# The first weight's fp16 parts without POOL, the low part of P in column halves, and a plan with new times

## Chip, core and metric

The kernel runs on one core of a Trainium2 chip. The metric is the device time of one execution in microseconds; it is given as the median of several runs.

## What is computed

Clustered attention is followed by a feed-forward block. The attention has 4 batches, 8 heads, 768 positions and a head dimension of 64. Cut to what matters:

```
q_assign = argmax(q_n . c_n)      # each query's cluster, of 16; k_assign likewise
mask     = q_assign == k_assign
scores   = where(mask, q k^T / 8, -1e9)
attn     = softmax(scores)
x        = (attn v) laid out as 3072 tokens x 512
h        = x @ w_in               # 512 x 2048
g        = h * tanh(softplus(h))
out      = g @ w_out              # 2048 x 512
```

## The kernel before

**Precision by two fp16 parts.** Nearly every matmul operand after the scores is split into a high fp16 part and a low fp16 part (what is left over), and products of parts are summed in PSUM. A feed-forward product takes three matmuls: high x high, high x low and low x high (lines 687 to 689 for w_in, 725 to 727 for w_out).

**Units.** The work of attention is cut into 96 units: 32 pairs of batch and head, three blocks of 256 queries each. A unit has two halves `a` of 128 queries. For each half TensorE makes scores (lines 520 and 525), VectorE the row's maximum (`rowmax`, line 535), ScalarE the exponentials P and their sum l (`expo`, line 542), and `recip` turns l into a factor (lines 552 and 553; the first step of it on POOL or VectorE). The page and the views call VectorE DVE, ScalarE ACT and GpSimd POOL.

- In the first 24 units (batch 0) P stays fp32 and is transposed on TensorE (line 581) and copied out of PSUM by DVE (line 600) or ACT (line 602). `pv` then multiplies it with an fp32 V of 64 columns (line 620). Two units share one PSUM bank: one writes partitions 0 to 63, the other 64 to 127. Their matmuls stand in turn in the queue, so each uses 64 of the array's columns ("128*64" in the profile). Line 641 spreads the factors in the same manner.
- In the other 72 units `p_hi` and `p_lo` make the parts of P (lines 571 and 588), one DMA transposes both, and `pv` runs once for two units, 36 times in all: for each unit 12 matmuls of line 630, six blocks of keys by two parts of P. The stationary operand is 128 columns wide, V's high part and V's low part side by side; the moving one is 256 queries. Rows 0 to 63 of the result hold what V's high part gives, rows 64 to 127 what its low part gives, and `pv_out` adds the two (lines 664 and 665).

**The weights.** `w_load`, `w_abs` (ACT, line 243) and `w_f32` (DVE, lines 256 and 258) turn 32 tiles that arrive as 64-bit words into fp32; `w_sq` sums their squares on TensorE (line 273) for a scale. Then come, for each of 16 column blocks, `w_hi` and `w_lo`, the fp16 parts. Blocks 0 to 7 are w_in, 8 to 15 w_out. There are two ways for a block. In one, POOL writes both parts (lines 297 and 306) after a scaling on POOL or ACT (lines 294 and 296). In the other, ACT writes the high part (line 291) and DVE the low part (line 304). The table's `f_w` says how many blocks go the second way; before, none of the first weight's did. `w_hi` of a block overwrites what `w_lo` of the block ahead of it has read, so the steps alternate.

**The order.** `Plan` holds each step with a due time, counted in units. `run` issues the steps in the order of these times, each after what it needs, and a scheduler then lays down each engine's queue from that. The times, and the shares of the steps that go to one engine or another (`share`: a share of 1 or more, or of -1 or less, takes every one), stand in the table `T` at the end of the file. Steps of the feed-forward are due one for each unit from 25.4 on; what is left of them when attention ends runs alone at the end.

Of the kernel before, what the change touches and what calls it, by code (L numbers as in the profile page):

```python
# [18 lines left out]
B, H, S, D, NCL = 4, 8, 768, 64, 16  # L19
# [36 lines left out]
def tile_clustered_attention_mish_ffn(  # L56
# [9 lines left out]
    nc = tc.nc  # L66
# [20 lines left out]
    st = {}  # L87
# [32 lines left out]
    units = [(g, qb, g) for g in range(NG) for qb in range(3)]  # L120
# [188 lines left out]
    vst = {}  # L309
# [245 lines left out]
    def mode(i, a):  # L555


        n, late = 2 * i + a, i >= T["units0"]
        if i < 3 * H:
            return 3  # L560
        return 2 if share(n, "f_lo", late) else int(share(n, "f_hi", late))
# [46 lines left out]
    def pv(m):  # L608

        for i in (2 * m, 2 * m + 1):  # L610
            b, h = divmod(units[i][0], H)
            pl.after(("ptrans", i, 0), ("ptrans", i, 1), ("v_split", b, h // 2))
        o = ps2.tile([P, 512], F32, tag="M", name=f"o{m}", bufs=1)
        early = mode(2 * m, 0) == 3
        if early:

            for c in range(6):
                for s in range(2):
                    b, h = divmod(units[2 * m + s][0], H)
                    nc.tensor.matmul(  # L620
                        o[s * D : s * D + D, :256], vst[b, h // 2][:, c, h % 2], st["pt", 2 * m + s][:, :, c, :],
                        start=(c == 0), stop=(c == 5), skip_group_check=True,
                    )
        else:

            for s in range(2):
                b, h = divmod(units[2 * m + s][0], H)
                for c in range(6):
                    for part in range(2):
                        nc.tensor.matmul(  # L630
                            o[:, s * 256 : s * 256 + 256], vst[b, h // 2][:, c, h % 2].rearrange("p g d -> p (g d)"),
                            st["pt", 2 * m + s][:, :, c + 6 * part, :],
                            start=(part == 0 and c == 0), stop=(part == 1 and c == 5), skip_group_check=True,
                        )
        if early:

            for s in range(2):
                for a in range(2):
                    pl.after(("recip", 2 * m + s, a))
                    c0 = 256 + a * P  # L640
                    nc.tensor.matmul(
                        o[s * D : s * D + D, c0 : c0 + P], st["l", 2 * m + s, a].to_broadcast([P, D]), ident,
                        start=True, stop=True, skip_group_check=True,
                    )
        st["o", m] = o
# [122 lines left out]
    for n in range(32):  # L768
        p = n // 16
# [5 lines left out]
    for i in range(16):  # L775
        p = i // 8
# [7 lines left out]
    for n in range(1, NG):  # L784

        span = T["span", int(n >= H)]
# [25 lines left out]
    for i in range(NU):  # L812
        for a in range(2):
            pl.at(i + T["scores", a], scores, i, a)
            pl.at(i + T["rowmax", a], rowmax, i, a)
            pl.at(i + T["expo", a], expo, i, a)
            pl.at(i + T["recip", a], recip, i, a)
            q = "q" if mode(i, a) == 3 else "p"
            pl.at(i + T[f"{q}_hi", a], p_hi, i, a)
            pl.at(i + T[f"{q}_lo", a], p_lo, i, a)  # L820
            pl.at(i + T[f"{q}_trans", a], ptrans, i, a)
        if i % 2:
            pl.at(i + T["pv"], pv, i // 2)
            pl.at(i + T["pv_out"], pv_out, i - 1)
            pl.at(i + T["pv_out"], pv_out, i)
# [17 lines left out]

T = {
    ('f_ws', 0): 0.5,
    ('f_ws', 1): 0.5,
    'direct': 2,
    'free': 6,
    't0': 2.1861,
    ('f_pl', 0): 0.5,  # L850
    ('as_o', 0): 0,
    ('as_o', 1): 0,
# [6 lines left out]
    ('dq', 'copy_z'): 0,  # L859
    ('dq', 'copy_b'): -9,  # L860
    ('dq', 'copy_a'): 0,
    ('f_copy_t', 0): 0,
    ('f_copy_z', 0): 0.567,
    ('f_copy_b', 0): 0,
    ('f_copy_a', 0): 0,
    ('f_copy_t', 1): 3,
    ('f_copy_z', 1): 0.874,
    ('f_copy_b', 1): 0,
    ('f_copy_a', 1): 0.193,
    ('f_a', 0): 1,  # L870
    ('f_a', 1): 0.239,
    ('f_b', 0): -1,
    ('f_b', 1): 0,
    'prep_hi': 3.0343,
    'prep_lo': 1.1321,
    'copy_t': 0.5952,
    'copy_z': 0.8008,
    'copy_b': 3.5728,
    'copy_a': 1.7632,
    'hot_copy': 0.979,  # L880
    'm_store': 0.3296,
    ('f_l', 0): 0,
    ('f_l', 1): 0.434,
    ('w_l', 0): 0.8888,
    ('w_l', 1): 0.7772,
    'v0': 2.031,
    'v_d': 0.4275,
    ('q_hi', 0): 0.8,
    ('q_lo', 0): 1.4045,
    ('q_trans', 0): -0.3083,  # L890
    ('q_hi', 1): 1.3,
    ('q_lo', 1): 1.5418,
    ('q_trans', 1): 1.5,
    ('f_w', 0): 0,
    ('f_w', 1): 0.363,
    'lead': 0.5333,
    'units0': 24,
    ('f_d', 0): 0.965,
    ('f_d', 1): 0.732,
    ('f_lo', 0): 0,  # L900
    ('f_lo', 1): 0,
    ('f_hi', 0): 0,
    ('f_hi', 1): 1,
    'grp': 2,
    'mish': 0,
    'O': 1,
    'off0': 25.401,
    'pace': 1.0,
    ('span', 0): 1.1575,
    ('span', 1): 1.0762,  # L910
    ('load', 0): -3.8837,
    ('load', 1): 2.8849,
    ('w0', 0): 0.89,
    ('w0', 1): 9.896,
    ('w_d', 0): 0.3597,
    ('w_d', 1): 0.1964,
    ('ws0', 0): 4.1159,
    ('ws0', 1): 1.7919,
    ('ws1', 0): -0.216,
    ('ws1', 1): 2.5545,  # L920
    ('ws_d', 0): 0.7109,
    ('ws_d', 1): 1.2087,
    'assign': 0.2164,
    'hot': 2.2946,
    'put': 2.3669,
    ('scores', 0): 0.4,
    ('rowmax', 0): 0.9821,
    ('expo', 0): 2.0645,
    ('recip', 0): 0.7,
    ('scores', 1): 1.8591,  # L930
    ('rowmax', 1): 1.6368,
    ('expo', 1): 1.1,
    ('recip', 1): 1.0726,
    ('p_hi', 0): 0.611,
    ('p_lo', 0): 0.9,
    ('p_trans', 0): 1.0,
    ('p_hi', 1): 1.3,
    ('p_lo', 1): 1.2157,
    ('p_trans', 1): 1.5,
    'pv': 3.4,  # L940
    'pv_out': 3.6,
    'm2': 4.327,
    'm_out': 0.4,
}

# [27 lines left out]
```

## Time and profile before

| | us |
|---|---|
| median of 3 runs (970.0 to 970.25) | 970.15 |
| the profiled execution | 970.7 |
| its span, first to last instruction | 968.9 |

So 1.8 us of the profiled execution lie outside its span, and it took 0.55 us longer than the median. A line of a view that groups instructions gives the source line, engine, operation, output and input, shapes and count; then the busy time in us and the mean duration of one in ns; then the idle time of the engine just before them and what ended it. "PEld" is TensorE's weight load. Matmuls are pipelined, so the duration of one is longer than the distance to the next one; the distance is what a stream of them costs. Shapes of a matmul are rows*columns of the array, then partitions x elements of the output or of the moving operand.

### The profile page before, as it was taken

The page shows a single profiled execution, that of the slowest core. Times are in us where ns is not written, and L with a number is a line of the kernel's source. Part 1 is how long each engine was busy: PE and PEld are TensorE (multiplying, and loading weights), DVE is VectorE, ACT ScalarE, POOL GpSimd, SP SyncE. Part 2 cuts the span into 40 slices and gives each one's busy share as a digit, 9 for nine tenths or more (in the row PEclk, how much of TensorE's full clock was granted, in tenths as well). Part 3 has the DMA queues.
Part 4 walks back from the last instruction along what each step waited for, and adds up shares of the span by engine and source line. Part 5 has one row for each costly group of instructions (what it writes and reads, how often), then busy time and mean ns, then how long its engine had stood idle before and what let it go on. Part 6 is the DMA issues. An engine that isn't in the chain of part 4 may idle for free. (4 is left out here: it accounts for less than half of the span.)

```text
span 968.9 us, 17115 instructions
## 1 busy us (share of the span) xinstructions
PE 906.2 (94%) x6385; PEld 668.9 (69%) x6385; DVE 648.8 (67%) x1169; ACT 554.2 (57%) x940; POOL 410.8 (42%) x542
## 2 busy tenths in 40 slices
PE   4788679999899999999999999899999999999997
PEld 3665456777677777667777767677777777666663
DVE  6897997887777767867776767877777766111010
ACT  4666367777666766566677656566666664211111
POOL 3227749744354444544444335544444343211110
PEclk9999789999999999999999999999999999999999
DMA  9733542246777857577785766578778666000000
GB/s 359 252 85 89 178 127 63 70 101 120 148 158 135 162 114 145 124 125 149 122 161 127 156 136 146 100 143 127 151 129 131 125 107 114 25 12 23 12 12 22
DMA packets 256083, 115.85 MB, mean 120 GB/s; under 512 B 230592, under 2 KB 236352, under 8 KB 256000
## 3 DMA queue, kind: packets, MB, share of 16 engines
q1 hardware_dynamic: 244320, 83.29, 43.8%
q10 hardware_dynamic: 11680, 31.46, 12.0%
q8 instruction: 50, 0.82, 0.4%
q14 instruction: 33, 0.27, 0.1%
HBM read 35.68 MB, written 6.29 MB: 43 GB/s over the span
## 5 line engine op out<-in xcount | busy, mean ns | idle before, releaser
L542 ACT ACTIVATE p<-s,m 128x768 f32<-128x768 f32 x192 | 172.9, 901 | 131.9 <-DVE m L535 108.2
L688 PE MATMUL h<-x,w 128*128 128x256 f16 x768 | 209.9, 273 | 1.1 <-POOL x L669 1.1
L687 PE MATMUL h<-x,w 128*128 128x256 f16 x768 | 210.0, 274 | 0.5 <-ACT u L697 0.5
L689 PE MATMUL h<-x,w 128*128 128x256 f16 x768 | 210.2, 274 | 0.0
L588 DVE SCALAR_TENSOR_TENSOR hl<-p,l,hl 128x768 f16<-128x768 f32 x144 | 152.8, 1063 | 64.2 <-POOL hl L571 63.3
L535 DVE TENSOR_REDUCE m<-s 128x1 f32<-128x768 f32 x192 | 181.1, 945 | 6.0 <-PE s L525 4.9
L571 POOL TENSOR_SCALAR hl<-p,l 128x768 f16<-128x768 f32 x144 | 133.5, 928 | 115.6 <-ACT p L542 38.2
L709 DVE SCALAR_TENSOR_TENSOR g<-u,mscg,g 128x512 f16<-128x512 f32 x96 | 76.2, 796 | 139.0 <-POOL g L701 138.4
L701 POOL TENSOR_SCALAR g<-u,mscg 128x512 f16<-128x512 f32 x96 | 82.4, 859 | 174.4 <-ACT u L697 148.9
L725 PE MATMUL O<-w,g 128*128 128x512 f16 x384 | 146.3, 381 | 2.2 <-POOL g L701 1.4
L727 PE MATMUL O<-w,g 128*128 128x512 f16 x384 | 145.7, 379 | 0.2 <-DVE g L709 0.2
L726 PE MATMUL O<-w,g 128*128 128x512 f16 x384 | 145.7, 380 | 0.0
L520 PE MATMUL s<-A,B 128*128 128x384 f32 x384 | 122.5, 400 | 15.5 <-ACT p L542 12.9
L697 ACT ACTIVATE u<-h,msch 128x512 f32<-128x512 f32 x96 | 65.8, 687 | 98.5 <-PE h L689 93.2
L630 PE MATMUL o<-pt,v 128*128 128x256 f16 x864 | 103.2, 273 | 1.0 <-DMA pt<-hl 0.4
L525 PE MATMUL s<-Z,T 80*128 80x384 f32 x384 | 100.5, 344 | 2.5 <-issue 1.9
L552 POOL TENSOR_SCALAR l<-l 128x1 f32<-128x1 f32 x129 | 39.6, 307 | 148.5 <-ACT p L542 145.2
L630 PEld LDWEIGHTS <-v 128*128 128x128 f16 x864 | 83.9, 98 | 18.5 <-issue 2.0
L687 PEld LDWEIGHTS <-w 128*128 128x128 f16 x768 | 75.3, 98 | 19.4 <-issue 5.5
L520 PEld LDWEIGHTS s<-A,B 128*128 128x128 f32 x384 | 63.3, 193 | 34.6 <-ACT p L542 20.0
L688 PEld LDWEIGHTS <-w 128*128 128x128 f16 x768 | 75.4, 98 | 17.0 <-issue 2.8
L689 PEld LDWEIGHTS <-w 128*128 128x128 f16 x768 | 75.4, 98 | 14.9 <-issue 5.4
(184 smaller groups left out, 1300.2 us busy)
## 6 DMA issues: line engine op xcount, KB each, us to landing
qk<-in_qk_dram ACTq DMA_DIRECT2D x30, 384.0 KB, 4.1
stage<-in_w_out_dram ACTq DMA_DIRECT2D x16, 512.0 KB, 4.9
vraw<-in_vP_dram SPq DMA_DIRECT2D x16, 384.0 KB, 4.0
out_dram<-osb SPq DMA_DIRECT2D x24, 256.0 KB, 2.2
B<-T ACTq DMA_DIRECT2D x30, 192.0 KB, 4.2
A<-A SPq DMA_DIRECT2D x25, 192.0 KB, 4.8
stage<-in_w_in_dram SPq DMA_DIRECT2D x8, 512.0 KB, 8.6
stage<-in_w_in_dram ACTq DMA_DIRECT2D x8, 512.0 KB, 4.6
```

The costliest lines, as they stand in the source:

```text
L520: nc.tensor.matmul(s[:, j, :384], st["B", n][:, q0 : q0 + P], st["A", n][:, j * 384 : (j + 1) * 384], start=True, stop=False,)
L535: nc.vector.tensor_reduce(m, st["s", i, a][:, :, :384], axis=AX.XY, op=ALU.max, negate=True)
L542: in_turn(nc.scalar.activation(p.rearrange("p (n x) -> p n x", n=2), st["s", i, a][:, :, :384], AF.Exp, bias=st["m", i, a], scale=1.0, acc ...
L571: nc.gpsimd.tensor_scalar(t[:, 0], p, r, 1.0, op0=ALU.mult, op1=ALU.mult)
L588: nc.vector.scalar_tensor_tensor(t[:, 1], p, r, t[:, 0], op0=ALU.mult, op1=ALU.subtract)
L630: nc.tensor.matmul(o[:, s * 256 : s * 256 + 256], vst[b, h // 2][:, c, h % 2].rearrange("p g d -> p (g d)"), st["pt", 2 * m + s][:, :, c + ...
L687: nc.tensor.matmul(o, wh, xh, start=(c == 0), stop=False)
L688: nc.tensor.matmul(o, wh, xl, start=False, stop=False)
L689: nc.tensor.matmul(o, wl, xh, start=False, stop=(c == 3))
L725: nc.tensor.matmul(o, gh, wh, start=(f == 0 and fi == 0), stop=False)
L726: nc.tensor.matmul(o, gh, wl, start=False, stop=False)
L727: nc.tensor.matmul(o, gl, wh, start=False, stop=(f == 7 and fi == 1))
```

## The change

In `pv`, for the 72 later units, the two kinds of matmul are parted. The 12 with P's high part stay as they were, those of the first unit and then those of the second. The 12 with P's low part take V's high part alone, a stationary operand of 64 columns, and the two units stand in turn: the first writes partitions 0 to 63, the second 64 to 127, each in its own 256 columns of the bank. The product of the two low parts is no longer computed. Only the first matmul of a block now starts the bank afresh, and the first of the second unit is placed behind it.

```diff
+            vs = [vst[b, h // 2][:, :, h % 2] for b, h in (divmod(units[2 * m + s][0], H) for s in range(2))]
+            pts = [st["pt", 2 * m + s] for s in range(2)]
             for s in range(2):
-                b, h = divmod(units[2 * m + s][0], H)
                 for c in range(6):
-                    for part in range(2):
-                        nc.tensor.matmul(
-                            o[:, s * 256 : s * 256 + 256], vst[b, h // 2][:, c, h % 2].rearrange("p g d -> p (g d)"),
-                            st["pt", 2 * m + s][:, :, c + 6 * part, :],
-                            start=(part == 0 and c == 0), stop=(part == 1 and c == 5), skip_group_check=True,
-                        )
+                    mm = nc.tensor.matmul(
+                        o[:, s * 256 : s * 256 + 256], vs[s][:, c].rearrange("p g d -> p (g d)"),
+                        pts[s][:, :, c, :], start=(s == 0 and c == 0), stop=False, skip_group_check=True,
+                    )
+                    if c == 0:
+                        if s:
+                            behind(mm, begun, "one start for the bank")
+                        begun = mm.ins.name
+
+            for c in range(6):
+                for s in range(2):
+                    nc.tensor.matmul(
+                        o[s * D : s * D + D, s * 256 : s * 256 + 256], vs[s][:, c, 0],
+                        pts[s][:, :, 6 + c, :], start=False, stop=(c == 5), skip_group_check=True,
+                    )
...
-    ('f_w', 0): 0,
+    ('f_w', 0): -1.1885,
...
-    ('w_d', 1): 0.1964,
+    ('w_d', 1): 0.3635,
```

Of the table some 45 numbers change. Those that move work between engines give these counts in the built programs, before and after:

| what | before | after |
|---|---|---|
| fp16 parts of the first weight: POOL pairs of lines 297 and 306 / ACT and DVE pairs of lines 291 and 304 | 8 / 0 | 0 / 8 |
| the same for the second weight | 6 / 2 | 5 / 3 |
| scalings of the first weight, ACT line 296 / POOL line 294 | 4 / 4 | 0 / 0 |
| first step of `recip`, POOL / DVE | 129 / 63 | 103 / 89 |
| of these in the first 24 units | 48 / 0 | 13 / 35 |
| `p_hi`, POOL (line 571) / ACT (line 573) | 144 / 0 | 123 / 21 |
| copies between halves of an operand, ACT (line 407) / DMA (line 409) | 53 / 67 | 61 / 59 |

The number `w_d` is the distance in units between two tiles of a weight; for the second weight it grows from 0.1964 to 0.3635, so that its 16 tiles are spread over 5.5 units and no longer over 2.9.

TensorE, the end of one `pv` block (the ninth of the 36) and what follows it, before; `pt` is the transposed P of one unit, `o` the bank:

```order
L630 LDWEIGHTS v_2_2513
L630 MATMUL o_4282<-pt_4031,v_2_2513 128x256
L439 MATMUL as_4377<-C,qk_4375 128x128 x6
L520 MATMUL s_1_4384<-A_3811,B_3825 128x384 x2
L525 MATMUL s_1_4384<-Z_3827,T_3813 128x384 x2
L725 LDWEIGHTS g_3914
L725 MATMUL O_1_4023<-w_1348,g_3914 128x512
```

The same place after; lines behind the changed part of the file are 10 higher now (725 is 735), and line 641 is the new matmul with P's low part:

```order
L641 LDWEIGHTS v_2_2498
L641 MATMUL o_4269<-pt_3952,v_2_2498 64x256
L641 LDWEIGHTS v_2_2498
L641 MATMUL o_4269<-pt_4049,v_2_2498 64x256
L439 MATMUL as_4364<-C,qk_4362 128x128 x6
L520 MATMUL s_1_4371<-A_3800,B_3820 128x384 x2
L525 MATMUL s_1_4371<-Z_4008,T_3802 128x384 x2
L735 LDWEIGHTS g_3901
L735 MATMUL O_1_4001<-w_1491,g_3901 128x512
```

The block now ends in matmuls of 64 rows of output that alternate between the two units' `pt`; what follows stands as before. The 36 blocks hold 37 such stretches, since one is cut in two by other work.

VectorE from the second row maximum of unit 10 on, before; `w` and `stage` belong to the second weight here:

```order
L535 TENSOR_REDUCE m_1_1213<-s_1_1208 128x1
L256 TENSOR_SCALAR w_1097<-w_1097 128x512
L258 SCALAR_TENSOR_TENSOR w_1060<-stage_1021,w_1060 128x512
L256 TENSOR_SCALAR w_1097<-w_1097 128x512
L553 RECIPROCAL l_1_1073<-l_1_1073 128x1
L661 TENSOR_TENSOR xf_1_0_1144<-o_1108,rb_1145 64x256
L661 TENSOR_TENSOR xf_1_1_1148<-o_1108,rb_1145 64x256
L600 COPY pt_901<-q_1_3_1027 128x384
L258 SCALAR_TENSOR_TENSOR w_1097<-stage_1033,w_1097 128x512
L258 SCALAR_TENSOR_TENSOR w_1097<-stage_1058,w_1097 128x512
L256 TENSOR_SCALAR w_1157<-w_1157 128x512
```

VectorE from the same row maximum on, after (line 671 is the former 661):

```order
L535 TENSOR_REDUCE m_1_1188<-s_1_1183 128x1
L304 SCALAR_TENSOR_TENSOR w_274<-w_313,ws0r,w_274 128x1024
L671 TENSOR_TENSOR xf_1_0_1131<-o_1104,rb_1132 64x256
L671 TENSOR_TENSOR xf_1_1_1135<-o_1104,rb_1132 64x256
L600 COPY pt_897<-q_1_3_1023 128x384
L552 TENSOR_SCALAR l_0_1151<-l_0_1151 128x1
L256 TENSOR_SCALAR w_1137<-w_1137 128x512
L461 TENSOR_REDUCE Dm_1418<-as_1198 128x12
L600 COPY pt_1049<-q_0_3_1045 128x384
L553 RECIPROCAL l_0_1151<-l_0_1151 128x1
L304 SCALAR_TENSOR_TENSOR w_313<-w_401,ws0r,w_313 128x1024
L258 SCALAR_TENSOR_TENSOR w_1137<-stage_1057,w_1137 128x512
```

The first weight's low parts (line 304) and the first step of `recip` (line 552) now stand among fewer steps of the second weight (lines 256 and 258).

POOL around units 9 and 10, before; `w` with `ws0r` is the first weight:

```order
L294 TENSOR_SCALAR w_761<-w_761,ws0r 128x1024
L297 TENSOR_SCALAR w_278<-w_279 128x1024
L552 TENSOR_SCALAR l_0_1043<-l_0_1043 128x1
L306 TENSOR_TENSOR w_278<-w_279,w_278 128x1024
L552 TENSOR_SCALAR l_1_1073<-l_1_1073 128x1
L297 TENSOR_SCALAR w_279<-w_318 128x1024
L306 TENSOR_TENSOR w_279<-w_318,w_279 128x1024
```

POOL from unit 9 to unit 11, after:

```order
L552 TENSOR_SCALAR l_1_1067<-l_1_1067 128x1
L382 TENSOR_SCALAR qk_1196<-qk_1196,scq 128x768
L470 TENSOR_TENSOR D_1417<-D_1417,desc 128x192
L385 TENSOR_SCALAR A_1230<-qk_1196 128x768
L393 TENSOR_TENSOR B_1274<-qk_1196,A_1230 128x768
L552 TENSOR_SCALAR l_1_1284<-l_1_1284 128x1
```

The first weight's steps are gone from POOL; what is left there is the preparation of heads (lines 382, 385, 393 and 470) and some first steps of `recip`.

More of the change, by code (lines that the diff above doesn't have):

```diff
@@ L845 @@
     ('f_ws', 0): 0.5,
-    ('f_ws', 1): 0.5,
+    ('f_ws', 1): 0.4363,
     'direct': 2,
     'free': 6,
-    't0': 2.1861,
+    't0': 2.1267,
     ('f_pl', 0): 0.5,
@@ L861 @@
     ('dq', 'copy_a'): 0,
-    ('f_copy_t', 0): 0,
-    ('f_copy_z', 0): 0.567,
-    ('f_copy_b', 0): 0,
+    ('f_copy_t', 0): 0.8228,
+    ('f_copy_z', 0): 0.7194,
+    ('f_copy_b', 0): -0.2835,
     ('f_copy_a', 0): 0,
[L866 to L870, printed above, removed]
+    ('f_copy_t', 1): 3.1145,
+    ('f_copy_z', 1): 0.4969,
+    ('f_copy_b', 1): 0.4912,
+    ('f_copy_a', 1): 0.063,
+    ('f_a', 0): 1.1703,
     ('f_a', 1): 0.239,
-    ('f_b', 0): -1,
-    ('f_b', 1): 0,
+    ('f_b', 0): -0.6667,
+    ('f_b', 1): 0.0811,
     'prep_hi': 3.0343,
[L875 to L878, printed above, removed]
+    'prep_lo': 0.9239,
+    'copy_t': 0.6329,
+    'copy_z': 2.6274,
+    'copy_b': 3.9121,
     'copy_a': 1.7632,
[L880 to L885, printed above, removed]
+    'hot_copy': 0.8469,
+    'm_store': 0.7735,
+    ('f_l', 0): -0.7426,
+    ('f_l', 1): 0.3715,
+    ('w_l', 0): 0.4954,
+    ('w_l', 1): 0.9639,
     'v0': 2.031,
-    'v_d': 0.4275,
+    'v_d': -0.0579,
     ('q_hi', 0): 0.8,
-    ('q_lo', 0): 1.4045,
-    ('q_trans', 0): -0.3083,
-    ('q_hi', 1): 1.3,
+    ('q_lo', 0): 1.2969,
+    ('q_trans', 0): -0.3391,
+    ('q_hi', 1): 1.0306,
     ('q_lo', 1): 1.5418,
-    ('q_trans', 1): 1.5,
-    ('f_w', 0): 0,
-    ('f_w', 1): 0.363,
-    'lead': 0.5333,
+    ('q_trans', 1): 1.3379,
+    ('f_w', 0): -1.1885,
+    ('f_w', 1): 0.3848,
+    'lead': 0.5862,
     'units0': 24,
-    ('f_d', 0): 0.965,
+    ('f_d', 0): 1.7993,
     ('f_d', 1): 0.732,
@@ L901 @@
     ('f_lo', 1): 0,
-    ('f_hi', 0): 0,
-    ('f_hi', 1): 1,
+    ('f_hi', 0): 0.0015,
+    ('f_hi', 1): 0.8585,
     'grp': 2,
@@ L908 @@
     'pace': 1.0,
-    ('span', 0): 1.1575,
+    ('span', 0): 1.1886,
     ('span', 1): 1.0762,
-    ('load', 0): -3.8837,
+    ('load', 0): -3.9074,
     ('load', 1): 2.8849,
@@ L914 @@
     ('w0', 1): 9.896,
-    ('w_d', 0): 0.3597,
-    ('w_d', 1): 0.1964,
-    ('ws0', 0): 4.1159,
-    ('ws0', 1): 1.7919,
-    ('ws1', 0): -0.216,
+    ('w_d', 0): 0.3504,
+    ('w_d', 1): 0.3635,
+    ('ws0', 0): 4.159,
+    ('ws0', 1): 1.6482,
+    ('ws1', 0): 0.0548,
     ('ws1', 1): 2.5545,
@@ L922 @@
     ('ws_d', 1): 1.2087,
-    'assign': 0.2164,
+    'assign': 0.2109,
     'hot': 2.2946,
@@ L926 @@
     ('scores', 0): 0.4,
[L927 to L931, printed above, removed]
+    ('rowmax', 0): 1.0087,
+    ('expo', 0): 1.7919,
+    ('recip', 0): 0.8297,
+    ('scores', 1): 1.8567,
+    ('rowmax', 1): 1.5377,
     ('expo', 1): 1.1,
[L933 to L936, printed above, removed]
+    ('recip', 1): 1.0376,
+    ('p_hi', 0): 0.7018,
+    ('p_lo', 0): 0.9708,
+    ('p_trans', 0): 1.179,
     ('p_hi', 1): 1.3,
@@ L940 @@
     'pv': 3.4,
-    'pv_out': 3.6,
-    'm2': 4.327,
+    'pv_out': 3.6154,
+    'm2': 4.1369,
     'm_out': 0.4,
```

## The prediction

> **What bounds the kernel now.** I read the page's first part, then the busy time by stage, then the groups by line, and the timeline where a duration was needed. The page, engine by engine:
>
> ```profile
> PE 906.2 (94%) x6385; PEld 668.9 (69%) x6385; DVE 648.8 (67%) x1169; ACT 554.2 (57%) x940; POOL 410.8 (42%) x542
> ```
>
> The stages (the columns are the stage, its length, then busy us of PE, PEld, DVE, ACT and POOL, the granted clock, the DMA share and GB/s):
>
> ```profile
> 0.00:85.00 85.00, 63.16 (x431) 49.09 (x431) 70.12 (x171) 49.13 (x99) 28.62 (x62) 0.94 0.61 206
> 85.00:145.00 60.00, 42.08 (x279) 29.44 (x279) 55.07 (x77) 30.86 (x58) 41.44 (x36) 0.83 0.51 148
> 145.00:220.00 75.00, 71.95 (x532) 55.44 (x532) 62.07 (x133) 55.08 (x109) 52.20 (x64) 1.00 0.35 77
> 220.00:830.00 610.00, 595.30 (x4259) 448.06 (x4258) 441.98 (x766) 396.98 (x642) 270.61 (x356) 1.00 0.71 134
> 830.00:968.90 138.90, 133.74 (x893) 86.87 (x890) 19.53 (x26) 22.20 (x34) 17.96 (x26) 1.00 0.04 16
> ```
>
> From 220 us on TensorE is nearly never idle: 14.7 us of 610, then a tail in which it works almost alone. Attention shares that stretch with the feed-forward, so a microsecond less TensorE work there ends the kernel a microsecond earlier, as long as no other engine takes over; DVE at 72% and ACT at 65% are the next. Before 220 us it is otherwise. From 85 to 145 us TensorE idles 17.9 us of 60 and DVE is busy 55.07, or 92%: that stage belongs to DVE. Stages add, since what is not idle on TensorE must be done at some time: the end is its work plus its idle time.
>
> **Part one, the column halves.** The groups of `pv`, and the timeline's rows of one late block and of one early block, which already works in column halves (start, us from there to the end of the last, count behind the x):
>
> ```profile
> L630 PE MATMUL o<-pt,v 128*128 128x256 f16 x864 | 103.2, 273 | 1.0 <-DMA pt<-hl 0.4 <-ACT stg L493 0.4
> L630 PEld LDWEIGHTS <-v 128*128 128x128 f16 x864 | 83.9, 98 | 18.5 <-issue 2.0 <-DMA pt<-hl 0.9
> L620 PEld LDWEIGHTS o<-pt,vraw 128*64 128x64 f32 x288 | 20.9, 137 | 12.8 <-issue 4.3 <-ACT stg L493 0.3 <-ACT pt L602 0.2
> ```
>
> ```profile
> 402.12 2.69 PE L630 MATMUL o<-pt,v 128*128 128x256 f16 x23
> ```
>
> ```profile
> 150.46 2.59 PE L620 MATMUL o<-pt,vraw 128*64 128x256 f32 x21
> ```
>
> ```profile
> 152.67 0.38 PE L620 MATMUL o<-pt,vraw 128*64 128x256 f32 x1
> 152.79 0.27 PE L641 MATMUL o<-ident,l 128*64 128x128 f32 x1
> 152.90 0.59 PE L641 MATMUL o<-ident,l 128*64 128x128 f32 x4
> 153.41 0.44 PE L520 MATMUL s<-A,B 128*128 128x384 f32 x1
> ```
>
> A late block's 23 matmuls take 2.69 us, of which the last takes 0.273: 22 distances in 2.42 us, 0.110 us each, so 24 cost 2.64 us. Of the early block 21 matmuls of 256 columns take 2.59 us; the last is 0.38 long (152.67), so ten pairs start within 2.21 us, 0.22 us a pair. Alone, an fp32 matmul of 128 columns stands 0.11 us from the next (152.79 to 152.90), so one of 256 would need 0.22: the two halves of the array run side by side, two for the price of one. The last of the four matmuls of 152.90 starts at 153.22 (0.59 less 0.27), and the full-width matmul behind it comes 0.19 us later where 0.11 would be usual: a change of width costs 0.08, and I take 0.09 each way, since the rows are rounded.
>
> So a new block costs 12 x 0.110 + 6 pairs x 0.110 + 2 x 0.09 = 2.16 us instead of 2.64. That is 0.48 us less; 36 blocks give 17.3, and the one that is cut in two costs two more changes, 0.2. I take **-17.1 us**. No row shows an fp16 pair. The lower bound of a pair is 0.110, since its 256 columns must stream. A dearer one would be bound by its loads: at the 0.137 of an fp32 load of 64 columns it costs 36 x 6 x 0.027 = 5.8 more, and with no overlap at all, 0.220, it costs 23.8 more, a loss of 6.7. I take 0.110, because the row of line 620, the nearest one, hides a 0.137 load behind each matmul.
>
> Two rules of the Trainium skill speak against this. "TensorEngine Tiling (Array Packing)", Restrictions, says that column tiling turns the fast weight load off; the trace has 137 ns for 64 fp32 columns beside 98 for 128 fp16 ones, so it does not contradict, and the dearer pair above is what that would make. "TensorE: Matmul & The Clock Gate", section The mechanism, says that a load overlaps running matmuls only where the row groups differ; here both halves use all rows. By that rule no load would be hidden, which is the last rival below; the rows of 402.12 and 150.46 speak against it, since they show loads under matmuls of the same rows.
>
> A result of the first unit is now complete only with its sixth pair, just before the second's. Its way out through ACT and DVE loses up to 12 x 0.110 = 1.3 us of head start. The matmuls queued behind are feed-forward and cover that; the next block stands two units behind, some 17 us by 610 us for about 72 units.
>
> **Part two, the first weight without POOL.** DVE in 0 to 85 us and in 85 to 145 us, POOL in the second, then the price of the new ways:
>
> ```profile
> L258 DVE SCALAR_TENSOR_TENSOR w<-stage,w 128x512 uint32<-128x512 uint32 x16 | 13.8, 877 | 0.0
> L256 DVE TENSOR_SCALAR w<-w 128x512 uint32<-128x512 uint32 x16 | 6.4, 417 | 0.2
> ```
>
> ```profile
> L258 DVE SCALAR_TENSOR_TENSOR w<-stage,w 128x512 uint32<-128x512 uint32 x16 | 20.1, 1267 | 0.1
> L256 DVE TENSOR_SCALAR w<-w 128x512 uint32<-128x512 uint32 x16 | 16.3, 1016 | 2.4 <-ACT w L243 2.3
> ```
>
> ```profile
> L306 POOL TENSOR_TENSOR w<-w,w 128x1024 f16<-128x1024 f32 x8 | 18.7, 2336 | 0.4
> L297 POOL TENSOR_SCALAR w<-w 128x1024 f16<-128x1024 f32 x8 | 9.8, 1225 | 0.4
> L294 POOL TENSOR_SCALAR w<-w,ws0r 128x1024 f32<-128x1024 f32 x4 | 4.4, 1127 | 0.1
> ```
>
> ```profile
> L304 DVE SCALAR_TENSOR_TENSOR w<-w,ws1r,w 128x1024 f16<-128x1024 f32 x2 | 2.9, 1450 | 0.0
> L552 DVE TENSOR_SCALAR l<-l 128x1 f32<-128x1 f32 x63 | 9.5, 152 | 15.0 <-ACT p L542 14.7
> L395 DVE SCALAR_TENSOR_TENSOR B<-qk,scq,A 128x768 fp32r<-128x768 f32 x24 | 26.2, 1090 | 0.3 <-POOL A L385 0.3
> L291 ACT ACTIVATE w<-w,ws1r 128x1024 f16<-128x1024 f32 x2 | 2.3, 1150 | 1.6 <-POOL w L306 1.5
> L296 ACT ACTIVATE w<-w,ws0r 128x1024 f32<-128x1024 f32 x4 | 4.3, 1138 | 1.1 <-DVE ws0r L206 1.1
> ```
>
> ```profile
> DVE l L553 <- POOL l L552: 8.7, 10, 2.9
> ```
>
> The same 32 DVE steps cost 20.2 us while POOL is mostly idle and 36.4 while it writes the first weight's parts (32.9 us of POOL): the two engines slow each other. Removed on DVE: that difference, 16.2 us, and of the 8.7 us of waits for POOL's step of `recip` (last row, before 220 us) the 35 of 48 that move, 6.3. Added: 8 x 1.45 = 11.6 for the low parts, 35 x 0.152 = 5.3 for `recip`, and by the queue's order three preparations of 1.09 that come before unit 22, 3.3. Sum: -16.2 - 6.3 + 11.6 + 5.3 + 3.3 = **-2.3 us**. DVE sets the pace there, so I let it count in full. ACT gets 8 x 1.15 and loses 4 x 1.14, 4.6 us more in all, in a stage where it is busy 30.86 of 60; but now ACT and DVE wait for each other block by block, and the exponentials are queued behind. Bounds: with none of the relief, +20.2; below, the jam of this stage:
>
> ```profile
> 94.05 0.94 DVE L535 TENSOR_REDUCE m<-s 128x1 f32<-128x768 f32 x1
> 95.25 2.60 DVE L258 SCALAR_TENSOR_TENSOR w<-stage,w 128x512 uint32<-128x512 uint32 x1
> 120.25 1.81 DVE L535 TENSOR_REDUCE m<-s 128x1 f32<-128x768 f32 x2
> ```
>
> ```profile
> 97.91 0.61 PE L273 MATMUL gram<-w 128*128 128x128 bf16 x4 [2.94 <-DVE w L258]
> 120.38 0.61 PE L273 MATMUL gram<-w 128*128 128x128 bf16 x4 [4.58 <-DVE w L258]
> ```
>
> For 26 us no row maximum is taken, and TensorE waits for weights. The wider `w_d` spreads these weights over nearly twice the units; if the jam goes whole, TensorE's idle time of the stage goes, -17.9.
>
> **Part three, the later units.** ACT takes over 21 high parts and, net, 8 copies:
>
> ```profile
> L387 ACT ACTIVATE A<-qk,scq 128x768 fp32r<-128x768 f32 x18 | 16.8, 935 | 17.8 <-PE s L520 17.6
> L407 ACT CAST Z<-B 64x768 fp32r<-64x768 f32 x24 | 19.9, 831 | 4.8 <-POOL B L393 3.4 <-DVE B L395 0.8
> ```
>
> 21 x 0.935 + 8 x 0.831 = 26.3 us more ACT, so (397 + 26) of about 593, or 71%. It stays off the bound. Yet TensorE's cover shrinks while the other engines' work grows. Its 14.7 us of waits may rise: from -5, if the new times remove some, to +14.7, if they double. I take **+2**.
>
> **The sum.** 970.7 - 17.1 - 2.3 + 2 = 953.3 for a profiled execution; the median lay 0.55 below it: **952.8 us**.
>
> **Rivals.**
> - The jam goes whole: -17.9 instead of -2.3, 937. For it: the spacing, and POOL's absence from the stage. Against: DVE still has as much work there.
> - Loads bound the pairs at 0.137: 5.8 more, 958.6. For it: only fp32 pairs have been seen.
> - The other engines follow less well and TensorE's waits after 220 us double: 12.7 more, 965.5. For it: rows of ACT and DVE at 71 to 75%. Against: each of them still idles for a quarter of that stage.
> - Slower: the fp16 halves do not run side by side. The low part then costs as before, the width changes come on top: 23.8 more, 976.6. It decides from a pair of about 0.19 us on (0.110 + 17.4/216, with 216 pairs). Against: line 620.
> - Slower: every load of 64 columns stands alone: 12 x 0.137 = 1.64 us a block more, 59 in all, 1012. This is what the rule on loads and row groups would make.
>
> **How the numbers follow.** The forecast has 0.52 and lies between 946 and 960: its third term down to -5, or its second up to +5, about a third of the way to its bound. The jam's end has 0.13, the loads 0.12, the doubled waits 0.10, the serial halves 0.07, the loads alone 0.02. The 0.04 left is for gains eaten wholly by waits, no change. A measurement of this kernel can tell 0.2%, 1.9 us, from no change. Faster is 0.52 + 0.13 + 0.12 + 0.10 = 0.87; the same 0.04; slower 0.09. The range 941 to 966 holds the forecast, the loads, the doubled waits and the jam going by three quarters; outside lie the rest of the jam, no change and both slower cases, under 0.2 in all.
>
> **What would show it.** In the profile after, the new low-part group should show pairs starting 0.11 us apart and PE's matmuls of `pv` falling from 2.64 to about 2.16 us a block. The stage from 85 to 145 us should show lines 256 and 258 near 0.42 and 0.88 us and line 273 waiting less. ACT should rise to about 71% between 220 and 830 us with TensorE's idle time there near 17 us. The prediction is wrong if pairs start 0.19 us or more apart, if TensorE's idle time before 220 us grows by more than the halves save, or if its waits after 220 us grow past 30 us.

## The result and the profile after

| | before | after |
|---|---|---|
| median of 7 runs each, us | 970.15 (969.5 to 970.63) | 966.12 (960.35 to 968.33) |
| the profiled execution, us | 970.7 | 966.99 |
| its span, us | 968.9 | 965.2 |

The ratio is 0.9949, with a 95% interval of 0.9926 to 0.9973: faster by 4 to 5 us, where 952.8 was forecast. After's own runs differ by 8 us, along with the granted clock: 960.35 us came at 0.990, 968.33 us at 0.979. One execution of a later kernel (line 688 left out), 975.13 us at a clock of 0.842, is left out of that kernel's numbers, since its three others had 0.951 to 0.969.

The page's line of the engines after:

```profile
PE 899.0 (93%) x6385; PEld 647.4 (67%) x6385; DVE 637.0 (66%) x1205; ACT 584.1 (61%) x974; POOL 346.6 (36%) x470
```

The stages after, columns as before:

```profile
0.00:85.00 85.00, 65.13 (x439) 51.07 (x441) 70.31 (x193) 54.92 (x106) 19.07 (x44) 0.92 0.60 202
85.00:145.00 60.00, 52.10 (x385) 38.47 (x382) 58.52 (x125) 46.65 (x88) 12.32 (x16) 0.94 0.51 152
145.00:220.00 75.00, 66.63 (x470) 49.66 (x469) 56.98 (x119) 51.75 (x95) 38.53 (x40) 0.93 0.30 68
220.00:830.00 610.00, 585.10 (x4232) 423.51 (x4229) 432.45 (x748) 410.14 (x658) 259.56 (x346) 0.99 0.69 133
830.00:965.20 135.20, 130.04 (x870) 84.67 (x867) 18.69 (x24) 20.63 (x30) 17.13 (x25) 1.00 0.04 14
```

From 85 to 145 us TensorE does 10 us more and VectorE 125 steps instead of 77 in the same time. From 220 to 830 us TensorE is idle for 24.9 us, not 14.7. The groups of `pv` in the whole kernel after:

```profile
L630 PE MATMUL o<-pt,v 128*128 128x256 f16 x432 | 55.4, 273 | 1.8 <-ACT stg L493 1.8
L641 PE MATMUL o<-pt,v 128*64 128x256 f16 x432 | 30.7, 277 | 0.0
L641 PEld LDWEIGHTS <-v 128*64 128x64 f16 x432 | 20.8, 109 | 7.9 <-issue 7.9
```

Together 86.1 us of matmuls where line 630 alone had 103.2: 17.1 us less. That sum overstates the gain, since a group's busy time counts the last matmul of each stretch at its full 0.27 us. From the first start of a whole block to the start of what follows it, the traces have 2.62 us before and 2.18 after (medians of the 23 blocks that nothing interrupts): 0.44 us less, or about 15.7 for 36 blocks. The page agrees with neither: all of TensorE's busy time falls by only 7.2 us, from 906.2 to 899.0. The timeline of one block after (nine matmuls of its first part, then the twelve with P's low part, then the next scores):

```profile
482.87 1.15 PE L630 MATMUL o<-pt,v 128*128 128x256 f16 x9
483.94 0.85 PE L641 MATMUL o<-pt,v 128*64 128x256 f16 x12
484.72 0.62 PE L520 MATMUL s<-A,B 128*128 128x384 f32 x2
```

Nine starts 0.11 us apart; then 483.75 to 483.94 is the first change of width, 0.19; then six pairs in 0.85 - 0.28 = 0.57 us between first and last start, 0.11 a pair; then 484.51 to 484.72, 0.21, the second change. That is nearly the block that was forecast: 2.16 us there, 2.18 here.

VectorE from 85 to 145 us after:

```profile
L258 DVE SCALAR_TENSOR_TENSOR w<-stage,w 128x512 uint32<-128x512 uint32 x16 | 12.1, 758 | 0.0
L304 DVE SCALAR_TENSOR_TENSOR w<-w,ws0r,w 128x1024 f16<-128x1024 f32 x8 | 11.8, 1471 | 0.0
L256 DVE TENSOR_SCALAR w<-w 128x512 uint32<-128x512 uint32 x16 | 7.2, 448 | 0.2 <-ACT w L243 0.2
```

Lines 258 and 256 took 1267 and 1016 ns there before: 16 x 0.509 + 16 x 0.568 = 17.2 us less. What TensorE waits for from 220 to 830 us, first before, then after (us in total, times, the longest):

```profile
PE s L520 <- ACT p L542: 7.6, 9, 2.6
```

```profile
PE s L520 <- ACT p L542: 13.7, 14, 2.3
PE s L525 <- DMA Z<-stg: 2.1, 2, 1.2
PE O L735 <- POOL g L711: 2.1, 3, 1.3
```

Its waits for the exponential, which frees the scores' bank, have almost doubled. To compare kernels I use two landmarks on VectorE, the row maximum that opens unit 24 and the one that opens unit 95. Before, then after:

```profile
203.67 0.95 DVE L535 TENSOR_REDUCE m<-s 128x1 f32<-128x768 f32 x1
...
814.87 0.94 DVE L535 TENSOR_REDUCE m<-s 128x1 f32<-128x768 f32 x1
```

```profile
192.77 0.96 DVE L535 TENSOR_REDUCE m<-s 128x1 f32<-128x768 f32 x1
...
811.81 0.94 DVE L535 TENSOR_REDUCE m<-s 128x1 f32<-128x768 f32 x1
```

The early units end 10.9 us earlier, and the later ones take 619.0 us instead of 611.2: 7.8 are given back, although the blocks of `pv` cost TensorE some 13 us less there.

### The profile page after: what moved, and what is told of

Same layout as the page of the kernel before. It is cut to its first block, busy times and chain, and to the rows that moved or that the text cites. A ratio compares the mean times of both kernels' runs of the same rounds, so it can differ in the third digit from the quotient of the medians.

```text
span 965.2 us, 17093 instructions
## 1 busy us (share of the span) xinstructions
PE 899.0 (93%) x6385; PEld 647.4 (67%) x6385; DVE 637.0 (66%) x1205; ACT 584.1 (61%) x974; POOL 346.6 (36%) x470
## 5 line engine op out<-in xcount | busy, mean ns | idle before, releaser
L571 POOL TENSOR_SCALAR hl<-p,l 128x768 f16<-128x768 f32 x123 | 113.8, 926 | 103.5 <-DVE l L553 36.2
L711 POOL TENSOR_SCALAR g<-u,mscg 128x512 f16<-128x512 f32 x96 | 77.5, 808 | 192.2 <-ACT u L707 169.7
L525 PE MATMUL s<-Z,T 80*128 80x384 f32 x384 | 102.7, 349 | 2.7 <-DMA Z<-stg 2.1
L525 PEld LDWEIGHTS s<-Z,T 80*128 80x128 f32 x384 | 71.8, 195 | 4.0 <-issue 3.2
L737 PEld LDWEIGHTS <-g 128*128 128x128 f16 x384 | 37.6, 98 | 47.9 <-DVE g L719 3.7
```

Of the source, the lines that this page charges most:

```text
L525: nc.tensor.matmul(s[:, j, :384], st["T", n][: D + NCL, q0 : q0 + P], st["Z", n][: D + NCL, j * 384 : (j + 1) * 384], start=False, stop=True,)
L571: nc.gpsimd.tensor_scalar(t[:, 0], p, r, 1.0, op0=ALU.mult, op1=ALU.mult)
L737: nc.tensor.matmul(o, gl, wh, start=False, stop=(f == 7 and fi == 1))
```

## The experiments

Theory A: the later units are held by the chain of scores, row maximum, exponential and parts of P, run in the engines' order, and that chain is as long as TensorE's own work, so what TensorE saves there becomes waiting. Theory B: the halves would pay, but the new times eat it. Theory C: the 21 high parts that moved to ACT eat it. All ratios are to the kernel before on the same chip; the two kernels of the second row ran on different chips, so that row compares less closely. Pairs with and without the halves, all else equal, came out so:

| the rest of the kernel | without halves | with halves |
|---|---|---|
| before's times | 1 | 1.0009 [1.0000, 1.0017] |
| first weight alone | 0.9923 [0.9904, 0.9942] | 0.9933 [0.9916, 0.9950] |
| all new times (first weight among them) | 0.9991 [0.9981, 1.0001] | 0.9949 [0.9926, 0.9973] |
| VectorE lighter | 1.0009 [0.9976, 1.0041] | 0.9926 [0.9897, 0.9956] |
| ScalarE lighter | 0.9848 [0.9825, 0.9872] | 0.9819 [0.9790, 0.9848] |
| first weight, copies by DMA | 1.0567 [1.0544, 1.0591] | 1.0360 [1.0325, 1.0395] |
| first weight, A on POOL | 0.9985 [0.9973, 0.9998] | 0.9958 [0.9942, 0.9974] |

**The halves alone** (`pv` of after, table of before).

```diff
-    ('f_w', 0): -1.1885,
+    ('f_w', 0): 0,
...
-    ('w_d', 1): 0.3635,
+    ('w_d', 1): 0.1964,
```

> The column halves alone, with the table of before. In the profile after, the pairs start 0.109 us apart and a change of width costs 0.093, so TensorE has 16.5 us less to do. Theory A (the other engines set the pace of the later units, and saved TensorE time comes back as its waits): the kernel gains only 2 to 6 us, 964 to 968, and TensorE's idle time between 220 and 830 us grows from 14.7 to 25 or more. Theory B (the halves pay in full and the new table gives it back in the later units): 952 to 956, with idle time near 15.

Measured: 970.99 us against 969.8. The landmarks and the stage:

```profile
203.84 0.95 DVE L535 TENSOR_REDUCE m<-s 128x1 f32<-128x768 f32 x1
...
815.81 0.94 DVE L535 TENSOR_REDUCE m<-s 128x1 f32<-128x768 f32 x1
```

```profile
220.00:830.00 610.00, 585.44 (x4254) 425.97 (x4252) 445.66 (x766) 395.96 (x642) 272.87 (x357) 1.00 0.69 133
```

Theory A had allowed a gain of 2 to 6 us; there is none. The later units take 612.0 us, as before (611.2), with all of before's times. From 220 to 830 us TensorE is busy for 9.9 us less and idle for 9.9 us more. Between the landmarks, counted from each matmul's start to the next one's, `pv` takes 13 us less (34 of its 36 blocks lie there, some of them interrupted), TensorE's other matmuls 4 more and its waits 10 more. So most of the saving is idle time; why the other matmuls take 4 us more is not shown. TensorE's longest waits from 220 to 830 us:

```profile
PE s L520 <- ACT p L542: 11.3, 13, 2.2
PE s L520 <- issue: 3.5, 2, 2.1
```

The waits for the exponential have grown from 7.6 to 11.3 us. The longest of them has its reason in ACT's queue; first ACT, then PE:

```profile
641.09 0.40 ACT L678 CAST x<-xf 128x256 f16<-128x256 f32 x1 [0.63 <-DVE xf L675]
641.52 0.69 ACT L707 ACTIVATE u<-h,msch 128x512 f32<-128x512 f32 x1
642.22 1.28 ACT L542 ACT_TABLE_LOAD   x1
643.52 0.90 ACT L542 ACTIVATE p<-s,m 128x768 f32<-128x768 f32 x1
```

```profile
644.56 0.62 PE L520 MATMUL s<-A,B 128*128 128x384 f32 x2 [2.22 <-ACT p L542]
```

The exponential that frees the bank stands behind a copy that waited for VectorE, a step of the feed-forward and a table load, and TensorE waits 2.22 us for it. Since the halves gain nothing even with before's times, theory B is not needed for that.

One rival stays untested. In the new block the first unit's result is complete later than before, as one block shows:

```profile
402.82 1.47 PE L630 MATMUL o<-pt,v 128*128 128x256 f16 x12
404.22 0.85 PE L641 MATMUL o<-pt,v 128*64 128x256 f16 x12
```

Both units' results end 2.25 us after the block's start; before, the first unit's ended with its 12 matmuls, after 1.47. The prediction took that as covered by the feed-forward; no run tells what these 0.8 us cost in the engines behind.

**The new times alone** (`pv` of before, table of after).

```diff
-                    mm = nc.tensor.matmul(
-                        o[:, s * 256 : s * 256 + 256], vs[s][:, c].rearrange("p g d -> p (g d)"),
...
+                    for part in range(2):
+                        nc.tensor.matmul(
```

> The new table alone, with the old matmuls. Theory A: the early units gain their 8 us and the later units stay as they were, 960 to 964. Theory B: the new table costs in the later units what the halves save, less the early gain: 978 to 984.

Measured: 969.15 us, in neither theory's range. Its later units take 618.9 us at a granted clock of 1.00 from 220 to 830 us, so the 0.99 of the kernel after is not why that kernel's take 619.0. With the next runs it says more than alone: the first weight is in this table too and is worth 0.9923 by itself, so the rest of the new times cost 0.0068, 6.6 us, where the halves are absent (the two ratios come from two chips).

**The halves and the first weight**, all other times as before.

```diff
-    ('f_w', 0): 0,
+    ('f_w', 0): -1.1885,
```

> The halves and the first weight's parts on ACT and DVE, all other numbers as before. The early stage should gain some 5 us or more over the halves alone, since DVE's steps of the second weight no longer meet POOL's. Theory A: 958 to 964. Theory B: 945 to 951.

Measured: 964.06 us. **The first weight alone**, the same line on the kernel before:

> The kernel before with the first weight's fp16 parts on ACT and DVE, and nothing else of the change: the share f_w of the first weight is -1.1885, pv stays as it was. Theory A (in the later units the chain of scores, row maximum, exponential and parts is as long as TensorE's work, so TensorE work taken away there turns into waits, and only the stage before unit 24 gets shorter by the first weight): as fast as halves and first weight together, whose ratio was 0.9933, so 0.990 to 0.996 of the kernel before, 961 to 966 us, with unit 24 reached about 10 us earlier than before. Rival D (halves and first weight need each other, since each alone leaves the other's engine as the bound): 0.998 to 1.000, 968 to 970 us. No theory has it below 0.989.

Measured: 961.7 us, the fastest of all kernels here that compute everything; its interval overlaps that of the pair. So the gain is the first weight's, and the halves add nothing. Up to the start of unit 24 (191.3 us here, 203.6 before) the busy times are, in the columns of the stages, first before, then here:

```profile
0.00:203.60 203.60, 160.79 (x1102) 120.35 (x1104) 173.99 (x354) 124.20 (x243) 115.53 (x151) 0.92 0.47 146
```

```profile
0.00:191.30 191.30, 155.29 (x1083) 118.22 (x1085) 161.70 (x360) 125.96 (x244) 82.01 (x130) 0.93 0.49 155
```

VectorE's busy time falls by 12.3 us and the stretch by 12.3, as it should if VectorE sets the pace there. Its steps on the second weight from 85 to 145 us:

```profile
L258 DVE SCALAR_TENSOR_TENSOR w<-stage,w 128x512 uint32<-128x512 uint32 x16 | 12.0, 753 | 0.1
L256 DVE TENSOR_SCALAR w<-w 128x512 uint32<-128x512 uint32 x16 | 6.6, 415 | 0.7 <-ACT w L243 0.6
```

These weights stand as close together as before, and yet TensorE's wait for them (line 273) falls from 13.2 to 0.9 us: moving the first weight off POOL is enough to end the jam. By unit 95 some 3 us are given back.

**High parts of P back on POOL**, else the kernel after.

```diff
-    ('f_hi', 1): 0.8585,
+    ('f_hi', 1): 1,
```

> The changed kernel with all high parts of P on POOL again (one number of the table). Theory C (the 21 high parts on ACT, 19.6 us of ACT's time, are what slows the later units): 954 to 959, TensorE's idle time between 220 and 830 us back near 15. Theories A and B: within 3 us of the changed kernel, 963 to 969.

Measured: 964.25 us, ratio 0.9951 [0.9933, 0.9969]; after has 0.9949. Theory C falls.

**VectorE lighter**, without and with the halves.

```diff
-            nc.vector.scalar_tensor_tensor(t[:, 1], p, r, t[:, 0], op0=ALU.mult, op1=ALU.subtract)
+            nc.vector.memset(t[:, 1], 0.0)
```

> The kernel before with DVE unburdened in the later units: the low part of P is a memset to zero instead of the subtraction of line 588, so the low part of the softmax is left out; TensorE has the same matmuls. It takes some 1.0 us off each of 144 steps of DVE and its waits for POOL's high part. It is the partner of the next run. By theory A (the chain through DVE, ACT and POOL sets the pace of the later units) it should be faster than before by up to the 14.7 us of TensorE's idle time: 955 to 966.

> The same memset in the kernel with the column halves alone. If DVE's queue is what set the pace (theory A with DVE), the halves now pay: 10 to 16 us less than the run before this one. If ACT's queue sets it, or if TensorE loses the time elsewhere, the two are within 4 us.

Measured: 970.6 and 962.04 us. A lighter VectorE alone brings nothing; with the halves, which alone bring nothing either, it brings 8 us. That fits theory A if two links must get shorter together, but neither forecast held: alone it was to gain, and 8 us lies between the two answers named for the pair. The ten executions of the first kernel also spread over 11 us.

**ScalarE lighter**, without and with the halves.

```diff
-        in_turn(nc.scalar.activation(st["u", j], st["h", j], AF.Mish, scale=vst[j // 24, "h"]))
+        in_turn(nc.scalar.activation(st["u", j], st["h", j], AF.Copy, scale=vst[j // 24, "h"]))
```

> The kernel before with ACT unburdened: Mish is replaced by a scaled copy, so the activation is left out, and with it 71 table loads of 1.28 us, 91 us of ACT's time. TensorE has the same matmuls. Partner of the next run. Theory A: 955 to 966.

> The same in the kernel with the column halves alone. If ACT's queue set the pace (theory A with ACT), 10 to 16 us less than the run before this one; if DVE's, within 4 us; if TensorE itself gives the saved time back, by changes of width or dearer matmuls elsewhere, within 4 us in this pair and in the other.

Measured: 953.52 and 950.11 us. The stage, without the halves and with them:

```profile
220.00:830.00 610.00, 607.67 (x4379) 459.51 (x4377) 453.75 (x774) 304.17 (x580) 270.23 (x362) 1.00 0.69 134
220.00:830.00 610.00, 603.25 (x4412) 440.93 (x4410) 452.39 (x772) 305.31 (x581) 271.22 (x362) 1.00 0.72 135
```

Without the table loads, 1.28 us each, TensorE is busy for 607.67 of 610 us and looks like the bound; the later units take 592.6 us. ACT's steps did hold them. The halves then bring 3 us more, and the two intervals overlap, so even that is not certain. This speaks against theory A as it stands: where TensorE is the bound, most of what the blocks save should come off. With the halves it waits 6.75 us, hardly for the exponential (0.2 us); why they pay so little here stays open, and the later result of the first unit may be part of it.

The Trainium skill, "ScalarE: Activation LUTs", section What ACT_TABLE_LOAD costs, gives 1.28 us for a load and 1.38 for a drain that goes with it. The rows of ACT above agree on the load, and show no drain: the step of line 707 ends at 642.21, the load starts at 642.22 and ends at 643.50, and the exponential starts at 643.52.

**More and less TensorE work.** Four matmuls more in each late block, then line 688 left out.

```diff
+                for c in range(2):
+                    nc.tensor.matmul(
+                        o[:, s * 256 : s * 256 + 256], vst[b, h // 2][:, c, h % 2].rearrange("p g d -> p (g d)"),
+                        st["pt", 2 * m + s][:, :, c, :], start=(c == 0), stop=(c == 1), skip_group_check=True,
+                    )
```

> The kernel before with four matmuls more in each of the 36 late blocks (their result is overwritten), 36 x 4 x 0.109 = 15.7 us more for TensorE, about what the halves take away. If TensorE set the pace of the later units, it would be 15.7 us slower, 985. If it and the chain through ACT and DVE are about equally long there (theory A at a corner, where less work gains nothing), more work must still cost nearly all of it: 979 to 986. If TensorE's time hardly matters either way: 970 to 974.

```diff
-                nc.tensor.matmul(o, wh, xl, start=False, stop=False)
```

> The kernel before without line 688, the product of w_in's high part with x's low part: 768 matmuls of 0.109 us, 84 us of TensorE, are left out; 576 of them, 63 us, stand beside the later units, 192, 21 us, in the tail. Theory A: the later units take nearly as long as before (unit 24's row maximum to unit 95's, 611 us before: 595 or more), since ACT and DVE pace them, and only the tail shrinks: 930 to 950. If TensorE sets the pace: 611 less 63 is 548, and the whole 970 less 84 is 886.

Measured: 988.79 us, ratio 1.0198 [1.0182, 1.0213], and 950.27 us, ratio 0.9797 [0.9777, 0.9816]. The first one's landmarks, then the second one's stage, landmarks and longest wait of TensorE:

```profile
203.75 0.95 DVE L535 TENSOR_REDUCE m<-s 128x1 f32<-128x768 f32 x1
...
831.70 0.94 DVE L535 TENSOR_REDUCE m<-s 128x1 f32<-128x768 f32 x1
```

```profile
220.00:830.00 610.00, 559.51 (x3661) 398.23 (x3660) 455.41 (x766) 394.23 (x639) 276.78 (x355) 0.96 0.68 134
```

```profile
204.31 0.95 DVE L535 TENSOR_REDUCE m<-s 128x1 f32<-128x768 f32 x1
...
818.88 0.94 DVE L535 TENSOR_REDUCE m<-s 128x1 f32<-128x768 f32 x1
```

```profile
PE s L520 <- ACT p L542: 30.8, 28, 3.0
```

This is the sharpest of the runs. TensorE sheds some 63 us in the later units (three quarters of 768 x 0.109) and they take 614.6 us, no less than before; the tail behind unit 95, where TensorE works almost alone, is 21.3 us shorter, and that is more than the whole gain. TensorE's waits for the exponential grow from 7.6 to 30.8 us and all its idle time from 14.7 to 50.5. The rest of the 63 us goes into matmuls that take longer, at a granted clock of 0.96 in this stage against 1.00 before; no run shows what the later units would take at 1.00. With 15.7 us more, they take 628.0, 16.8 more than before, and the kernel is slower than either forecast for it. So the kernel stands in a corner: TensorE's work added there counts in full, taken away it counts for nothing.

**Less work for both**: line 688 left out and ScalarE lighter, both edits above in one kernel.

> The same without line 688, and Mish replaced by a scaled copy, so that 91 us of table loads are gone from ACT. If ACT's queue is what paces the later units in the run before this one, they now fall well below its time, by 30 us or more. If DVE's and POOL's queues pace them, they stay within 15 us of it.

Measured: 906.83 us, ratio 0.9353 [0.9326, 0.9380]; the later units take 571.2 us. That is 43 us below the kernel that leaves out line 688 alone, as was expected if ACT's steps pace the later units. From the lighter ScalarE alone (592.6) 21 of TensorE's 63 us now count.

**Halves not in turn**: the low part of the first unit whole, then the second's.

```diff
-            for c in range(6):
-                for s in range(2):
+            for s in range(2):
+                for c in range(6):
```

> The column halves alone, with the low part's 12 matmuls ordered by unit, so that one half of the array works at a time: 0.109 us for each instead of for two, 0.65 us a block or 23.5 us in all more than the halves alone, and 7 us more than before for the changes of width. By theory A some of it is hidden as the halves' gain was: 972 to 980. If TensorE sets the pace: 977 and 23 us above the halves alone only if those had gained 16, which they did not.

Measured: 969.75 us, ratio 1.0008 [0.9998, 1.0018], less than the 972 to 980 expected. One block:

```profile
402.16 1.47 PE L630 MATMUL o<-pt,v 128*128 128x256 f16 x12
403.56 1.09 PE L641 MATMUL o<-pt,v 128*64 128x256 f16 x12
```

The low part takes 1.09 us here and 0.85 in turn. Some 9 us more TensorE work over 36 blocks change nothing in the time, as theory A has it.

**Which link of the chain?** Three edits on the kernel with the first weight alone; the first two were run with the halves as well. First, the copies of line 407 go through DMA.

```diff
-    ('dq', 'copy_t'): 3,
+    ('dq', 'copy_t'): 0,
...
-    ('f_copy_t', 1): 3,
-    ('f_copy_z', 1): 0.874,
+    ('f_copy_t', 1): 0,
+    ('f_copy_z', 1): 0,
```

> The kernel with the first weight's parts on ACT and DVE and pv as before, and now the copies between the halves of an operand (line 407) go to DMA in the later units: their count on ACT falls from 53 to about 8, 45 x 0.83 = 37 us less ACT work, the computation stays whole. Theory A1 (ACT's queue is the link of the chain that paces the later units): the later units take up to 16 us less, as they did when ACT lost its table loads, until TensorE is the bound: 950 to 960 us, TensorE over 98% busy from 220 to 830 us. Rival A2 (the chain's latency through DVE, DMA and POOL paces it, not ACT's load; the longer way of a DMA copy takes back what ACT gains): 962 to 970 us.

> The same with the column halves of pv added: both parts of the change that the runs so far have told apart, and ACT relieved of the copies, the computation whole. Theory A1: with ACT relieved TensorE is the bound, and its 16.5 us less work pay at least in part, 4 to 12 us below the same kernel without the halves: 942 to 955 us. Rival A2: no difference to the kernel without the halves beyond 2 us, 960 to 970 us.

Measured: 1024.9 and 1003.31 us; no theory had either. The chain of the first of them:

```profile
768.81 0.62 SPq L604
769.53 7.10 DMA Z<-B
776.73 0.47 ACTq L409
777.25 0.69 ACT u L697
```

The copy takes 7.10 us. The next copy is issued from ACT's queue (line 409), must wait for it, and all of ACT's work behind it waits too. So ACT got lighter and later at once, and the pair does not tell load from latency. Why the halves bring 20 us there, more than TensorE saves, stays open.

Second, POOL makes the first part of the operand A.

```diff
-    ('f_a', 1): 0.239,
+    ('f_a', 1): 1,
```

> The kernel with the first weight's parts on ACT and DVE and pv as before, in which POOL instead of ACT makes the first part of the operand A for the later heads (line 385 instead of 387, 18 times): 18 x 0.93 = 17 us less ACT work, without the longer way of a DMA. Theory A1 (ACT's queue paces the later units): 3 to 8 us less than the first weight alone, 953 to 959 us. Rival A2 (the latency of the chain through ACT, POOL and DVE paces it; POOL has these steps in its queue ahead of the high parts and slows DVE): 960 to 968 us.

> The same with the column halves of pv. Theory A1: the halves now pay, 2 to 8 us less than the same kernel without them. Rival A2: no difference beyond 2 us, either way.

Measured: 968.17 and 965.29 us. ACT's relief costs 6 us, against theory A1 and at the upper end of its rival's range. The halves then bring 2.6 us; that lies in A1's range, but the two intervals just touch.

Third, more work for ACT.

```diff
+        if j < 72:
+            more = mp.tile([P, 256], F16, tag="more", name=f"more{j}", bufs=1)
+            nc.scalar.activation(more, st["u", j][:, :256], AF.Copy)
```

> The kernel with the first weight's parts on ACT and DVE, and one more step on ACT behind each of the first 72 steps of line 697: a copy of 256 columns that nobody reads, 72 x 0.4 = 29 us of ACT work in the later units, in which ACT is idle for 220 us of 610. Theory A1 (ACT's queue paces the later units): 20 to 30 us more than the first weight alone, 982 to 992 us. Rival A2 (latency elsewhere in the chain): ACT's idle time takes most of it, 962 to 972 us.

Measured: 967.32 us, ratio 0.9979 [0.9968, 0.9991]: 5.4 us more than 0.9923. The stage with the first weight alone, then with the extra work:

```profile
220.00:830.00 610.00, 595.68 (x4245) 445.95 (x4243) 437.67 (x757) 390.71 (x634) 267.92 (x354) 1.00 0.70 132
```

```profile
220.00:830.00 610.00, 594.46 (x4233) 445.21 (x4233) 436.42 (x756) 415.65 (x706) 267.49 (x354) 1.00 0.70 132
```

ACT takes 25 us more, and four fifths of it vanish in its idle time. So ACT's sum of work is not the bound. What is left is the latency of the chain, with the waits of one in-order engine for another in it; no run shows that directly. That the table loads count because they stand in that chain fits these runs except for how little the halves bring beside a lighter ScalarE, but was not tried apart from the work that the lighter ScalarE also sheds.

## Why the prediction was wrong

**The step that failed** is the first one: "so a microsecond less TensorE work there ends the kernel a microsecond earlier, as long as no other engine takes over". No single engine took over: after, VectorE is busy for 71% of the stage and ScalarE for 67% (71% was forecast). What TensorE no longer did came back as its waits, more than half of the increase for the exponential; the runs fit a chain through several engines, and a lighter ScalarE does shorten it. The condition was judged by shares, VectorE 72% and ScalarE 65%, and shares don't show a chain in which the engines wait for each other in turn. With before's times and with the first weight alone the term of -17.1 us is worth 0; with the new times it is worth 4. The rival "TensorE's waits after 220 us double", 965.5 us at a chance of 0.10, came nearest in time and in sign: the waits for the exponential went from 7.6 to 13.7 us. It was judged by the same shares, and thought too unlikely for that.

**The signs.** None of the three signs by which the prediction was to be wrong came: pairs start 0.11 us apart, TensorE's idle time before 220 us falls from 42.8 to 36.1 us, and behind it the waits come to 24.9 us and not to 30. The last sign stood too high: the busy time of that stage falls by only 10.2 us, so that waits of 25 are enough to take all of it.

**Two misses that partly cancel.** By the landmarks the early units were to gain 2.3 us and the rest of the kernel 15.1. The early units gain 10.9, and the rest loses 7.2. Had the early units gained only the 2.3 us of the forecast, all else as measured, the kernel after would have been slower than before; that it came out faster owes nothing to the term that the forecast rested on.

**The halves themselves** were nearly right: 0.109 us a pair, about 0.20 us from the last matmul of one width to the first of the other, 0.09 more than in a stream. A whole block gets 0.44 us shorter, where 0.48 was forecast; that the sums of busy time differ by just 17.1 us is a coincidence. The loads of 109 ns are hidden. That runs against the rule of the Trainium skill, "TensorE: Matmul & The Clock Gate", section The mechanism, by which loads overlap only where row groups differ; here both halves use all rows. (The same section also lets a load run ahead when it goes to the background weight buffer, which would agree with the trace.) The serial rivals fall.

**The first weight** was right in kind and too small. Lines 256 and 258 fell by 17.2 us (16.2 forecast), line 304 takes 1.47 us in after (1.45 forecast) and 1.28 in the kernel with the first weight alone. Yet unit 24 starts 10.9 us earlier in after, and 12.4 with the first weight alone, instead of 2.3. Up to there VectorE's busy time falls by 7.3 us in after (174.1 to 166.8), where the sum has it grow by 4.0, and its idle time by 3.6, where the sum has 6.3. In after TensorE's wait for the second weight (line 273 for line 258) fell from 13.2 to 1.2 us in the stage from 85 to 145. The sum charged added steps in full: the 35 steps of line 552 were to cost 5.3 us, but overlap their neighbours and cover only 0.8 us in which VectorE does nothing else. And it did not price what a quieter POOL does for VectorE's other steps: line 473 takes some 3 us less up to unit 24. The rival of the jam, -17.9, had the mechanism more nearly.

**The later units** were to cost 2 us through ACT's load, 26.3 us more of it; it rose by 13.2. ACT's high parts are innocent. The rest of the new times costs 6.6 us without the halves and, after 0.9949 against 0.9933, 1.5 with them (these two intervals overlap).

## What to carry to other kernels

An engine that is busy 98% of a stage need not be worth relieving: take a large piece of its work away and add a piece, each in a kernel of its own, before counting a saving; here 63 us less in the later units did not shorten them and 15.7 us more cost 17. Where queues run in order, look for the chain that goes round the engines, and shorten it together with the busy engine or not at all. And take a many-part change apart: one number of the table, the first weight's, gives 0.9923 alone, as much as or more than the whole.

## What was not expected of the hardware

Two halves of 64 columns overlap even when they are not queued in turn: with all six matmuls of one unit ahead of the other's, the low part spans 0.82 us from first to last start, not the 12 x 0.109 = 1.3 us of a serial run. VectorE's steps on 128x512 words depend on POOL's company by more than I allowed: line 256 takes 1016 ns beside a busy POOL and 448 beside a quiet one, 415 where only the first weight was moved.
